# Hedgehog linear attention with a gated unit on one core: tiles 2 and 3 as two pairs of products, four down-weight loads behind the state, and a newly searched order

## The chip, the core and the metric

The kernel runs on one core of a Trainium2 chip. The metric is device time in microseconds (us) of one execution; a kernel's time is the median of its runs. The profile is of one execution, taken by the hardware profiler. A core has five engines with a queue of instructions each: TensorE (PE; its weight loads are PEld), VectorE (DVE), ScalarE (ACT), GpSimd (POOL) and SyncE (SP). Here SP issues nearly all DMAs. Products are collected in PSUM, in eight banks of 128 rows by 512 float32 values, numbered 0 to 7.

## The reference, cut to what matters

One block of a transformer on 2048 tokens of width 448, in bfloat16: an attention without a softmax over tokens (16 heads of 28), and then a gated unit of width 1792. Each half has a layer norm before it and a sum with its input after it.

```python
qkv = layernorm(x) @ wqkv                       # q, k, v: 16 heads, 28 wide
pq, pk = q @ w_phi, k @ w_phi                   # per head, 28 x 28
phi_q = concat(softmax(pq), softmax(-pq))       # over the 28 features
phi_k = concat(softmax(pk), softmax(-pk))
kv = einsum("bhsf,bhsd->bhfd", phi_k, v)        # the state: sums over all 2048 tokens
z  = einsum("bhsf->bhf", phi_k)
o  = (phi_q @ kv) / (phi_q . z + 1e-6)
h  = x + o @ wo
n  = layernorm(h)
out = h + (sigmoid(n @ w_gate) * (n @ w_up)) @ w_down
```

No query can be finished before the state `kv` holds all tokens. That splits the program into a part before the state and a part behind it.

## The kernel before, in words

The tokens are 16 tiles of 128. The kernel is a graph of tasks. A task has a name, an engine, a function that issues its instructions, and the tasks that it depends on. `stored` reads a table `ORDER` that is written in the file: each number holds a task (number divided by 32), the engine that it takes where several are allowed, and which of the allowed PSUM banks it uses. `emit` puts the tasks into the engines' queues in that order, and puts in a wait wherever a task depends on another engine. So nothing is decided at run time: the order of every queue, SP's too, is that of the table. A list `TURNS` adds single dependencies on top, each of one named task on another, all of them of a POOL task on a DVE task. The table came out of a search with a model of the engines; the search isn't part of the file.

The tasks that the change and the prediction speak of, in the order of the data (numbers in brackets are lines of the profile of before; copies by the helper `copy` all have line L432):

- **Loads** (L468), on SP: `x` in pieces (`x0` is tiles 0 and 1, `x2` 2 and 3, on ACT's queue, `x4`, `x6`, then `x8` and `x12` with four tiles each), `wk` (weights of the keys), `wph` (w_phi), `wv` (weights of the values, two halves), `wq` (of the queries, four pieces), `wom` (of the output, eight small pieces), later `wg`, `wu` (gate, up) and `wd` (down, seven pieces).
- **Norm of x**: statistics (`bst` L590, `agg` L592), the power -1/2 on POOL (`rstd` L595), normalised tiles `xn` (L610 on DVE, L609 on ACT). Tiles 0 to 3 are transposed on PE (L620) and copied out; tiles 4 to 15 go as six DMA transposes `xT` (L628), two tiles each.
- **Folded weights**: the key weights are multiplied by w_phi on PE (L547, L562) and copied out by ACT, giving `Wk2`; the same for the queries after two DMA transposes `wqT` (L508), giving `Wq2`. `fill` (L995) are products of zeros that write a bank nobody reads.
- **Keys and values** (L644): a pair of products of 448 columns for two banks. A pair is issued as two tasks, `pa` (8 matmuls) and `pb` (6). An ordinary pair holds keys and values of one tile. For a tile in the list `VV`, the pair `va`/`vb` holds the values of two tiles and `pa`/`pb` their keys. The second task of a pair waits until the first one has ended.
- **Features of the keys**: `ekp`, `ekm` (two exponentials on ACT, L664, L666), `v1` (values copied out), `ss` (sums, DVE, L685), `rs` (reciprocal, L689), `phi` (the product of the two, L691, on POOL or DVE), `kv` (16 matmuls into bank 4, L703), `kvz` (the state copied out of bank 4 by DVE, L758).
- **Queries** (L743): `qa`/`q`, two groups for each of four chunks of four tiles, with exponentials `eqp`, `eqm` on ACT (L753).
- **Output of the attention**, by tile: `num` (L779, 16 matmuls) and `ocp` (copied out). By pair of tiles: `rSm`, `rr`, `b`, `c`, `rd`, `o` on DVE (L795 to L807), `od` (L826), a DMA transpose `oT` (L828; pair 0 on PE with two copies `oT0.0` and `oT0.1`), `woa`/`wo_` (L840), `h` (the sum with x, L870; for pair 0 the copies `hc`), `bst2`/`agg2`, `ve2` and `rstd2` (POOL, L880), the normalised `hn` (L884), and a DMA transpose `hT` (L902; pair 0 on PE). `oT1` is of pair 1 (tiles 2 and 3), and so on.
- **Gated unit**, in five chunks of 2, 4, 4, 4 and 2 tiles, 14 columns of 128 each: `ga`/`gu` (L941, 8 and 6 matmuls; `gu5.1` is column 5 of chunk 1), `sig` (ACT, L950), `hh` (DVE, L958), then by tile `dn` (L975, 14 matmuls), `fin` (DVE, L982) and the store `st` (SP, L985).

Chunk 1 of the gated unit needs `hT1` and `hT2`, chunk 2 `hT3` and `hT4`, chunk 3 (tiles 10 to 13) `hT5` and `hT6`, chunk 4 `hT7`. The last chunk's `dn` close the program.

Of the kernel before, what the change touches and what calls it, by code (L numbers as in the profile page):

```python
# [32 lines left out]
NFILL = 12  # L33
# [53 lines left out]
"""  # L87


TURNS = [(('rstd', 4), ('xn', 3)), (('phi', 0), ('xn', 9)), (('phi', 4), ('xn', 12)), (('phi', 7), ('xn',  # L90
         15)), (('phi', 10), ('phi', 9)), (('phi', 14), ('phi', 13)), (('ve2', 2), ('hn', 3)), (('rstd2', 2),
         ('hn', 3)), (('ve2', 4), ('o', 5)), (('rstd2', 4), ('o', 5)), (('rstd2', 3), ('od', 5)), (('rstd2',
         5), ('od', 7))]


class _Task:
# [232 lines left out]
def build(nc, A_x, A_wqkv, A_w_phi, A_wo, B_w_gate, B_w_up, B_w_down, out):  # L329
    S = A_x.shape[1]  # L330
    NT = S // P
# [17 lines left out]
    with ExitStack() as es:  # L349
# [6 lines left out]
        phi = sb("phi", [P, NPHI, 2, 2 * G, 32, 2])  # L356
# [42 lines left out]
        kvz = sb("kvz", [P, 2, G, E, 2])  # L399
        opm = sb("opm", [P, NOP, 2, 2, G, E, HL])  # L400
        rSm = sb("rSm", [P, 2, 2, G, HL], dt.float32)
        rr = sb("rr", [P, 2, 2, G, HL])
# [633 lines left out]
```

## Time and profile before

| What | Value |
|---|---|
| Time, median of 3 runs (lowest to highest) | 205.77 us (205.53 to 206.45) |
| The profiled execution: its time, its span | 206.47 us, 204.7 us |
| Busy: PE, DVE, ACT, POOL | 196.0, 134.4, 94.7, 33.0 us |
| Granted TensorE clock | 0.998 |
| First pair on DMA-transposed tiles begins | 19.28 us |
| The last `kv` ends, the state is complete | 47.00 us |
| First `ga` of chunk 0, first `ga` of chunk 1 | 65.40, 78.66 us |
| First `dn` | 97.22 us |

The span runs from the first to the last instruction; the time of an execution has 1.77 us more around it here. In the profile a row of the timeline or of the chain begins with the start and the duration in us; a row of a group ends with its busy time in us, the mean duration of one instruction in ns, and the idle time of the engine just before. A matmul of a pair uses half of the rows of the array, and two of them run side by side, so that the busy time of one is about twice what it costs in the queue. Instructions that issue a DMA stand under the queue of their engine (SPq), and the time to landing counts from the start of the issue.

### The profile page before, as it was taken

To read this page: it belongs to the slowest core of one execution; us is meant where nothing else is said; L and a number is where in the kernel's file an instruction comes from. 1 tells how busy PE (TensorE), PEld (TensorE's weight loads), DVE (VectorE), ACT (ScalarE), POOL (GpSimd) and SP (SyncE) were. 2 spreads that over 40 slices of the span, in tenths; PEclk is the share of its full clock that TensorE was granted. 3 is DMA by queue.
4 is the path that set the end of the run, shared out by engine and by line. 5 is a ranking of instruction groups with operands and counts; after the bars stand their busy time and mean duration, and the time that the engine had idled before them with its cause. 6 is when DMAs were issued, how large, how long until landed. Compare 5 with 4: busy or idle time off the path is not lost.

```text
span 204.7 us, 5395 instructions
## 1 busy us (share of the span) xinstructions
PE 196.0 (96%) x2276; PEld 109.5 (53%) x2276; DVE 134.4 (66%) x304; ACT 94.7 (46%) x169; POOL 33.0 (16%) x51
## 2 busy tenths in 40 slices
PE   7996999998889998999999999999999999999994
PEld 2643545555436985554544555454444555786553
DVE  2969989997999995779948846713455313541412
ACT  2698999999999462444031441301334400441000
POOL 5515936570000200003000000110000000000000
PEclk9999999999999999999999999999999999999999
DMA  5999599574040396310260020050020000200041
GB/s 144 317 248 162 161 165 148 159 226 142 3 100 6 80 150 160 96 45 11 52 146 5 0 51 3 0 125 3 0 74 3 2 0 3 69 3 0 30 159 60
DMA packets 35109, 16.94 MB, mean 83 GB/s; under 512 B 26828, under 2 KB 34060, under 8 KB 35084
## 3 DMA queue, kind: packets, MB, share of 16 engines
q1 hardware_dynamic: 34812, 16.36, 35.3%
q8 instruction: 18, 0.29, 0.7%
q10 hardware_dynamic: 272, 0.23, 0.3%
q14 instruction: 7, 0.06, 0.1%
HBM read 8.98 MB, written 1.84 MB: 53 GB/s over the span
## 4 chain that ended last, share of the span: by engine, by line
PE 85%; DMA 5%; DVE 4%; SPq 3%; issue 1%; ACT 0%; DVEq 0%
PE bank L941 42%; PE bank L975 21%; PE bank L644 8%; PE bank L743 5%; PE bank L840 5%; SPq L468 3%; DMA x_sb<-in_A_x_dram 3%; PE bank L703 2%; DMA xnT<-xn_pad 2%; PE bank L779 1%; DVE o_pad L807 1%; DVE opm L432 1%; DVE st L865 1%; ACT opm L432 0%; DVE st L590 0%
## 5 line engine op out<-in xcount | busy, mean ns | idle before, releaser
L941 PE MATMUL bank<-xnT,wg_sb 64*128 64x512 bf16 (+1 forms) x490 | 87.5, 333 | 0.6 <-issue 0.6
L941 PE MATMUL bank<-xnT,wu_sb 64*128 64x512 bf16 (+1 forms) x490 | 87.6, 333 | 0.0
L950 ACT ACTIVATE sg_sb<-bank 128x512 f32<-128x512 f32 (+1 forms) x70 | 34.7, 512 | 81.9 <-PE bank L941 76.1
L958 DVE SCALAR_TENSOR_TENSOR hh<-sg_sb,bank 128x512 bf16<-128x512 f32 (+1 forms) x70 | 39.0, 575 | 30.8 <-ACT sg_sb L950 28.5
L941 PEld LDWEIGHTS bank<-xnT,wg_sb 64*128 64x128 bf16 x490 | 45.0, 94 | 21.3 <-issue 3.5
L941 PEld LDWEIGHTS bank<-xnT,wu_sb 64*128 64x128 bf16 x490 | 44.8, 94 | 14.0
L975 PE MATMUL bank<-wd_sb,hh 128*128 128x448 bf16 (+1 forms) x238 | 43.1, 342 | 0.0
L975 PEld LDWEIGHTS bank<-wd_sb,hh 128*128 128x128 bf16 x238 | 22.9, 98 | 20.1 <-DVE b_sb L799 0.4
L982 DVE SCALAR_TENSOR_TENSOR x_sb<-bank,x_sb 128x448 bf16<-128x448 f32 (+1 forms) x17 | 9.9, 594 | 24.6 <-PE bank L975 24.5
L644 PE MATMUL bank<-Wk,xnT 64*128 64x448 bf16 x112 | 21.7, 350 | 0.3
L644 PE MATMUL bank<-Wv,xnT 64*128 64x448 bf16 x112 | 21.9, 350 | 0.0
L691 POOL TENSOR_TENSOR phi<-ek,rsum 128x896 bf16<-128x896 bf16 x10 | 16.8, 1690 | 9.0 <-DVE xn_pad L610 4.8
L685 DVE TENSOR_REDUCE ssum<-ek 128x32 f32<-128x896 bf16 x16 | 16.6, 1068 | 0.9 <-ACT ek L664 0.7
L753 ACT ACTIVATE eq<-bank 128x1024 bf16<-128x1024 f32 x16 | 16.7, 1068 | 0.2
L880 POOL TENSOR_TENSOR rs<-rs,neghalf 128x2 f32<-128x2 f32 x8 | 5.6, 698 | 59.5 <-DVE rs L878 59.2
L743 PE MATMUL bank<-xnT,Wq 64*128 64x512 bf16 x112 | 14.3, 377 | 0.0
L840 PE MATMUL bank<-wo_sb,oT 64*128 64x448 bf16 x112 | 13.0, 350 | 0.6 <-DVE rs L878 0.6
L432 ACT CAST opm<-bank 128x960 bf16<-128x960 f32 x13 | 12.1, 976 | 1.4 <-PE bank L779 1.4
L644 PEld LDWEIGHTS bank<-Wk,xnT 64*128 64x128 bf16 x112 | 9.2, 94 | 6.0 <-PE bank L644 1.5
L644 PEld LDWEIGHTS bank<-Wv,xnT 64*128 64x128 bf16 x112 | 9.1, 94 | 4.9 <-ACT WkT L432 0.3
L870 DVE TENSOR_TENSOR x_sb<-bank,x_sb 128x896 bf16<-128x896 f32 x7 | 7.5, 1087 | 3.4 <-PE bank L840 3.4
L590 DVE BATCH_NORM_STATS2 st<-x_sb 128x6 f32<-128x448 bf16 x16 | 9.2, 604 | 0.5 <-DMA x_sb<-in_A_x_dram 0.5
(92 smaller groups left out, 168.3 us busy)
## 6 DMA issues: line engine op xcount, KB each, us to landing
wu_sb<-in_B_w_up_dram SPq DMA_DIRECT2D x4, 448.0 KB, 3.8
wg_sb<-in_B_w_gate_dram SPq DMA_DIRECT2D x4, 448.0 KB, 4.8
out_dram<-x_sb SPq DMA_DIRECT2D x15, 112.0 KB, 1.8
wd_sb<-in_B_w_down_dram SPq DMA_DIRECT2D x7, 224.0 KB, 2.8
x_sb<-in_A_x_dram SPq DMA_DIRECT2D x2, 448.0 KB, 5.4
x_sb<-in_A_x_dram SPq DMA_DIRECT2D x3, 224.0 KB, 4.3
wq_raw<-in_A_wqkv_dram SPq DMA_DIRECT2D x4, 128.0 KB, 3.5
Wv<-in_A_wqkv_dram SPq DMA_DIRECT2D x2, 224.0 KB, 4.5
```

The source lines that it names most:

```text
L432: return e.copy(dst, src) if hasattr(e, "activation") else e.tensor_copy(dst, src)
L644: r = e.matmul(bank[bk][:, 0:D], lhsT=half(xnT, hi)[:, t, k, :], rhs=half(w, hi)[:, k, :], start=(i == 0), stop=(i == 6), tile_position=(6 ...
L685: task(("ss", t), "dve", dve(896), lambda e, s=s: e.tensor_reduce(ssum[:, s, :].rearrange("p (a h) -> p a h", h=2), ek[:, s].rearrange("p ...
L691: task(("phi", t), None, 1.68, lambda e, t=t, s=s: e.tensor_tensor(phi[:, t % NPHI, :, :, 0:DH, :].rearrange("p a g d h -> p (a g) d h"), ...
L743: r = e.matmul(bank[bb[j]], lhsT=half(Wq2, hi)[:, k, 2 * g:2 * g + 2].rearrange("p c d h -> p (c d h)"), rhs=half(xnT, hi)[:, 4 * c:4 * c ...
L753: task((key, gp, c), "act", act_p(1024), lambda e, gp=gp, c=c, sg=sg, nm=nm: e.activation(eq[c][:, sg, 2 * gp:2 * gp + 2, :], wide[got(nm) ...
L840: r = e.matmul(bank[bb[j]][:, 0:D], lhsT=half(oT, hi)[:, pr % NO, j, k, :], rhs=half(wo_sb, hi)[:, k, :], start=(i == 0 and not res), stop ...
L941: r = e.matmul(bank[b][:, 0:N], lhsT=half(w, hi)[:, k, fs], rhs=half(hnT, hi)[:, t0:t0 + n, k, :], start=(i == 0), stop=(i == 6), tile_pos ...
L950: task(("sig", f_, c), "act", act_p(N), lambda e, j=j, N=N, nm=nm: e.activation(sg_sb[:, j % NSG, 0:N], bank[got(nm)[0]][:, 0:N], ACT.Tanh ...
L958: task(("hh", f_, c), "dve", dve(N), lambda e, j=j, N=N, nm=nm, f_=f_, c=c: e.scalar_tensor_tensor(hhT[c % 2][:, f_, 0:N], sg_sb[:, j % NS ...
L975: r = e.matmul(bank[b][:, c0:c1], lhsT=hhT[c % 2][:, f_, o:o + P], rhs=wd_sb[:, f_, c0:c1], start=(f_ == 0), stop=(f_ == FT - 1))
L982: task(("fin",) + nm[1:], "dve", dve(c1 - c0), lambda e, nm=nm, tt=tt, pr=pr, c0=c0, c1=c1: e.scalar_tensor_tensor(X(tt)[:, c0:c1], bank[g ...
```

## The change

Four things change in the code, and the table is replaced.

1. `VV` gets tile 2 as a second entry. Tiles 2 and 3 were two ordinary pairs; they become one pair of values (`va2`/`vb2`) and one pair of keys (`pa2`/`pb2`). Two dependencies that named `pb` of a tile now take it from `k_at`, since tile 3 no longer has a `pb` of its own.
2. The loads `wd0` to `wd3` depended on `gu1.0`, `gu3.0`, `gu5.0` and `gu7.0`; now they depend on `kvz`. Each load also waits for the one two places before it in the list of late loads, as before.
3. `NFILL` goes from 12 to 16.
4. `TURNS` has 8 entries in place of 12, of which most are new.
5. `ORDER` is new throughout: engines, banks and places in the queues.

```diff
-NFILL = 12
+NFILL = 16
...
-544 737 0 128 320 1152 448 609 352 27904 480 577 27936 512 768 160 9120 192 640 96 27968 224 288 28000 800 256
...
+544 737 0 224 128 1152 448 577 160 27904 352 609 96 27936 480 640 27968 512 192 256 28000 800 320 384 28032
...
-TURNS = [(('rstd', 4), ('xn', 3)), (('phi', 0), ('xn', 9)), (('phi', 4), ('xn', 12)), (('phi', 7), ('xn',
-         15)), (('phi', 10), ('phi', 9)), (('phi', 14), ('phi', 13)), (('ve2', 2), ('hn', 3)), (('rstd2', 2),
-         ('hn', 3)), (('ve2', 4), ('o', 5)), (('rstd2', 4), ('o', 5)), (('rstd2', 3), ('od', 5)), (('rstd2',
-         5), ('od', 7))]
+TURNS = [(('rstd', 2), ('xn', 1)), (('rstd', 4), ('xn', 2)), (('phi', 1), ('xn', 10)), (('phi', 5), ('xn',
+         15)), (('rstd2', 0), ('rr', 3)), (('rstd2', 2), ('od', 3)), (('rstd2', 1), ('hn', 4)), (('rstd2', 4),
+         ('c', 6))]
...
-        VV = (0,)
+        VV = (0, 2)
...
-                     ("gu", 1 + 2 * j, 0) if name[0] == "wd" else ("pb", 4 + 2 * j + (name[0] == "wu"))])
+                     ("kvz" if j < 4 else ("gu", 1 + 2 * j, 0)) if name[0] == "wd" else ("pb", 4 + 2 * j + (name[0] == "wu"))])
...
-                deps.append(("pb", min(4 * c + 3, NT - 1)))
+                deps.append(k_at[min(4 * c + 3, NT - 1)][2])
...
-            qdone = [("q", gp, c) for gp in range(2)] + [("pb", NT - 1)]
+            qdone = [("q", gp, c) for gp in range(2)] + [k_at[NT - 1][2]]
```

What the new table does to the queues, as far as the prediction speaks of it (before, then after):

```
SP, first loads   x0 wk1 wk0 x4 wph x6 wv1 wv0 wom0 wq3 wq2 wq1 wq0 x8 x12 wqT1 wqT0 xT4 xT6
                  x0 wk0 wk1 wph x6 x4 wq3 wq1 wq2 x8 wq0 wom2 wv1 wv0 x12 wqT1 wom1 wqT0 wom6 xT4 xT6
PE, tiles 0 to 3  va0 .. vb0 .. pa0 pb0 pa3 pb3 pa2 pb2
                  pa0 pb0 pa2 va0 pb2 va2 vb0 vb2
phi on DVE        3 5 8 9 13 15
                  0 2 4 9 10 11 14 15
SP, behind state  oT1 oT2 wd1 oT3 wd3 wd0 hT1 hT2 wd5 oT4 wd2 wd4 wd6
                  wd1 oT1 oT2 oT3 wd0 hT2 hT1 wd2 wd3 wd4 oT4 wd6 wd5
DVE, near chunk 3 hn13 hh8.2 hh10.2 hn12 hn10 fin4
                  hh13.2 hh11.2 hn14 hn15 fin3 hn12 hn13 fin4
SP, near chunk 3  oT7 hT6 hT5 st0 hT7 st1
                  oT7 st0 hT5 st3 st1 hT6 hT7
PE, near chunk 3  dn2 dn4 dn5 dn3, then chunk 3
                  dn2 dn3 dn4 dn5, then chunk 3
```

90 rows, old and new, of the table ORDER are left out of this document.

## The prediction

> **What bounds it now.** I read the busy shares first, then the busy time by stage (cut at the events of the table above), the chain that ended last in order of time, the waits, and last SP's queue and the landings of single DMAs.
>
> ```profile
> PE 196.0 (96%) x2276; PEld 109.5 (53%) x2276; DVE 134.4 (66%) x304; ACT 94.7 (46%) x169; POOL 33.0 (16%) x51
> ```
> ```profile
> 19.28:47.00 27.72, 27.72 (x486) 15.31 (x488) 25.61 (x49) 25.72 (x48) 18.19 (x14) 1.00 0.78 172
> 47.00:65.40 18.40, 16.23 (x330) 8.84 (x332) 17.51 (x41) 17.72 (x22) 0.70 (x1) 1.00 0.22 57
> 65.40:78.66 13.26, 12.64 (x244) 11.18 (x239) 12.45 (x36) 7.43 (x18) 1.59 (x3) 1.00 0.69 130
> 78.66:130.04 51.38, 51.38 (x473) 26.34 (x474) 37.34 (x82) 16.12 (x27) 2.93 (x5) 1.00 0.19 46
> 130.04:140.74 10.70, 10.70 (x58) 5.40 (x60) 3.76 (x9) 0.60 (x1) 0.76 (x2) 1.00 0.26 61
> ```
>
> The columns of the second fence are stretch, length, then busy time and count of PE, PEld, DVE, ACT, POOL. PE is the bound, and it has little left to give. From 19.28 to 47.00 it has no gap at all, and none from 78.66 to 140.74. It idles 18.40 - 16.23 = 2.17 us while the attention's output is begun, and 0.62 us before chunk 1. In those two stages, and from 19.28 on, DVE is nearly as full as PE (25.61 of 27.72, 17.51 of 18.40, 12.45 of 13.26). So DVE decides when the waits there end. PE's work does not change: the same 2 x 7 x 16 matmuls for keys and values, only paired otherwise.
>
> ```profile
> 8.35 5.29 DMA x_sb<-in_A_x_dram
> 14.85 4.39 DMA xnT<-xn_pad
> 78.04 0.62 issue
> 130.04 10.70 PE bank L975 x56
> ```
> ```profile
> PEld bank L644 <- PE bank L644: 1.5, 3, 0.5
> PE bank L562 <- DMA WqT<-wq_raw: 1.5, 1, 1.5
> PE bank L848 <- DVE oT L432: 0.6, 1, 0.6
> PE bank L840 <- DVE rs L878: 0.6, 1, 0.6
> ```
>
> The chain runs over the load x8, the statistics and the transpose xT4, which lands at 19.24; everything behind is PE. Where PE waits, it waits for a DMA transpose or for DVE.
>
> **The pairs of tiles 2 and 3: 0.** The waits show three weight loads that sat 0.5 us each until PE was empty: `pb` directly behind its own `pa`. In the new order only pb0 follows so. That saves two such stops, but ahead of the wait for WqT and xT4 (1.5 us of PE standing still at L562), which goes on as long as those transposes are in flight. Values don't start earlier either: pa0 and pa2 stand before va0, and Wv is now issued 13th and 14th. If the cover were gone, two stops would be worth up to 2 x 0.5 = 1.0 us.
>
> **Four more fills: 0.** They are short, stand in the same idle stretch, and only kT starts behind them; pa0 waits for ACT's copies of Wk2.
>
> **The start: +0.4 us.**
>
> ```profile
> 8.35 1.56 SPq L468 DMA_DIRECT2D x_sb<-in_A_x_dram  x2
> 10.31 4.49 SPq L508 DMA_TRANSPOSE WqT<-wq_raw  x2
> 14.85 3.26 SPq L628 DMA_TRANSPOSE xnT<-xn_pad  x2
> 18.16 1.66 SPq L468 DMA_DIRECT2D wo_sb<-in_A_wo_dram  x2
> ```
>
> x8 moves up four places, some 2 us at 8.35 us for the fourteen it had. That ends DVE's wait for it. But SP is busy without a hole from the WqT transposes into xT4 (10.31 + 4.49 = 14.80, then 14.85), so earlier `xn4` and `xn5` don't bring xT4 forward. Nearly the same bytes stand ahead of the WqT transposes as before. New are two pieces of `wo`: wom1 between the WqT transposes and wom6 between the second one and xT4. One piece costs SP 1.66 / 2 = 0.83 us. wom1 falls where the transposes are held back anyway (4.49 us for two), wom6 does not. Ends: -0.5 (SP is freed sooner, as DVE's wait for x8 was 0.5) and +0.83. I take +0.4, half a piece, since the landing of xT4 followed 4.4 us behind its issue and part of that is the queue of DMAs, not SP. PE has no gap behind 19.28, so this goes through to the state.
>
> **More on DVE before the state: 0, with ends 0 and +1.1.**
>
> ```profile
> L691 POOL TENSOR_TENSOR phi<-ek,rsum x10: 1689/1690/1691, 19.1 to 44.1; 128x896 bf16<-128x896 bf16 x10
> L691 DVE TENSOR_TENSOR phi<-ek,rsum x6: 558/587/834, 29.8 to 45.5; 128x896 bf16<-128x896 bf16 x6
> L432 DVE CAST v<-bank 128x448 bf16<-128x448 f32 x1 | 0.6, 626 | 0.5 <-PE bank L644 0.5
> ```
>
> DVE makes eight `phi` instead of six, and two copies of values instead of one: 2 x 0.587 + 0.626 = 1.8 us more. Its idle time in that stage was 27.72 - 25.61 = 2.1 us. It fits, with 0.3 us over, and phi15 and the last `kv` stay at the end of both queues.
>
> **From the state to chunk 1: -0.3 us.**
>
> ```profile
> L432 DVE CAST opm<-bank 128x960 bf16<-128x960 f32 x3 | 3.5, 1154 | 0.6 <-PE bank L779 0.6
> L432 DVE CAST x_sb<-bank 128x448 bf16<-128x448 f32 x1 | 0.6, 593 | 0.0
> L432 DVE COPY oT<-bank 128x512 bf16<-128x512 bf16 x1 | 0.4, 426 | 0.1
> L958 DVE SCALAR_TENSOR_TENSOR hh<-sg_sb,bank 128x256 bf16<-128x256 f32 x28 | 10.9, 414 | 7.2 <-ACT sg_sb L950 5.5 <-PE bank L975 1.6
> L878 DVE TENSOR_SCALAR rs<-mv 128x2 f32<-128x2 f32 x6 | 1.0, 165 | 0.1
> L880 POOL TENSOR_TENSOR rs<-rs,neghalf 128x2 f32<-128x2 f32 x8 | 5.6, 698 | 59.5 <-DVE rs L878 59.2 <-DVE o_pad L826 0.2
> ```
>
> Up to the last `hn` of tiles 2 to 5 DVE loses ocp8 (1.154) and hc0 (0.593) to ACT and gains oT0.0 (0.426), ve22 (0.165) and one more `hh` (0.414): -0.74. But hn0 now stands directly behind rstd2 of pair 0, which POOL makes in 0.698 and which was filled by ocp8: +0.7, and what stands behind hn0 waits too (hP0 on PE among it). So the last `hn` comes as before.
>
> Its transposes then meet the loads of `wd`:
>
> ```profile
> 71.18 1.05 SPq L468 DMA_DIRECT2D wd_sb<-in_B_w_down_dram  x2
> 72.48 3.88 SPq L902 DMA_TRANSPOSE xnT<-hn_pad  x2
> 132.09 2.59 SPq L902 DMA_TRANSPOSE xnT<-hn_pad  x2
> ```
> ```profile
> L902 SPq DMA_TRANSPOSE xnT<-hn_pad x2: 1231/1896/2561, 72.5 to 73.8; - x2
> ...
> DMA to landing us min/median/max: 4.8/5.0/5.3
> ```
> ```profile
> DMA to landing us min/median/max: 2.8/2.8/2.8
> ```
>
> The second fence is the tile `hn_pad` in 72 to 76 us, the third the same tile in 131 to 134. With two loads just ahead a transpose lands after 4.8 to 5.3 us, with none after 2.8. Now wd1 is issued before oT1 and out of the way, but wd0 still goes directly before hT2 and hT1; the new dependency on `kvz` does not move it, its place in the queue does. One load ahead instead of two is worth 1.05 / 2 = 0.5 us at most; and woa1 takes banks 2 and 3 and so no longer waits for hc0 (the second wait of 0.6 us above, whose named releaser stands directly behind hc0). Ends: -1.2 (both PE waits of 0.6 go) and +0.7 (POOL's 0.698 unpaid). I take -0.3, near the middle. `dn0` has its weights long before; that the loads come earlier is worth 0. wd1 waits on SP for `kvz` and for wu3, with oT1 behind it, but oT1 isn't ready before:
>
> ```profile
> 57.05 3.49 SPq L828 DMA_TRANSPOSE oT<-o_pad  x2
> ```
>
> That is 10 us behind the state: 0.
>
> **Before chunk 3: +0.5 us.**
>
> ```profile
> 135.48 0.62 DVE L982 SCALAR_TENSOR_TENSOR x_sb<-bank,x_sb 128x448 bf16<-128x448 f32 x1 [3.09 <-PE bank L975]
> 131.66 0.73 DVE L884 TENSOR_SCALAR hn_pad<-x_sb,mv,rs 128x512 bf16<-128x512 bf16 x2
> out_dram<-x_sb SPq DMA_DIRECT2D x15, 112.0 KB, 1.8
> ```
>
> So far hT5 and hT6 were issued at 132.09 and landed under the four `dn` (56 matmuls, 10.70 us). Now hn12 and hn13 stand behind fin3 on DVE, and fin3 waits for dn3; behind them wait hT6 and hT7: two `dn` take 10.70 / 2 = 5.35, fin3 0.62, the two `hn` 0.73, together 6.7 us behind the start of dn2; with st3 and st1 ahead on SP hT6 is issued about 7.3 us behind it. Landing after 2.8 us makes 10.1, in time for chunk 3 at 10.7. Landing after 5.3 us makes 12.6, 1.9 late. Ends 0 and +1.9; I take +0.5, because two stores of 112 KB are half of two `wd`.
>
> The Trainium skill (DMA: Bandwidth & Descriptors, Queues, rings and completion order) has each DMA engine take descriptors in ring order, without a barrier between the data of two DMAs. By that alone two stores would hold hT6 back by no more than their own bytes, and this term would be 0 and the sum 0.1. The 5.3 us behind two loads speak for more, so the row stands.
>
> **The sum:** 0 + 0 + 0.4 + 0 - 0.3 + 0.5 = +0.6 us. The profiled execution, 206.47, is 0.70 above the median; I put the 0.6 on the median: 206.4 us. What a measurement of this kernel can tell from no change is about 0.5%, 1.03 us.
>
> **Rivals.**
>
> *Slower, by hT6 (0.23).* If the transpose behind st3 and st1 lands after 5.3 us, PE stands 1.9 us before chunk 3, with the start's 0.4 and the -0.3: 207.8. For it speaks the landing behind `wd`; against it that stores land in 1.8. It decides from a landing of about 4.3 us on.
>
> *Slower, by POOL and DVE (0.15).* phi15 took 0.834 instead of 0.558 us:
>
> ```profile
> 44.14 1.69 POOL L691 TENSOR_TENSOR phi<-ek,rsum 128x896 bf16<-128x896 bf16 x1 [1.16 <-DVE phi L691]
> 45.47 0.83 DVE L691 TENSOR_TENSOR phi<-ek,rsum 128x896 bf16<-128x896 bf16 x1
> ```
>
> POOL's `phi` ran until 45.83, and DVE's ended 0.47 behind that. The turns that kept phi10 and phi14 on POOL behind DVE's are gone, and DVE has two more. One DVE `phi` that comes just behind POOL's start would stand up to 1.69 us; with 0.3 to spare this moves the state by 1.4: 205.77 + 0.6 + 1.4 = 207.8. Against it: by the new order POOL has no `phi` beside most of DVE's. The Trainium skill (SBUF — State Buffer, Who interferes with whom) says that a DVE instruction with two SBUF inputs and a GpSimd one that reads SBUF shut each other out for a whole instruction; by that rule the full 1.69 is possible, and the one row agrees.
>
> *Faster (0.20).* All transposes land in 2.8 us and DVE's -0.74 counts: the start -0.5, the stage before chunk 1 -1.2, chunk 3 nothing: 205.77 - 1.7 = 204.1.
>
> *As summed (0.42)*: 206.4, its own range 205.0 to 206.8. It holds too if the change does nothing, the tables being worth the same.
>
> **Range and chances.** From the faster case, 204.1, to the two slower ones, 207.9; beyond lie both slower ones together or a wait that I don't see. Faster by over 0.5%: 0.20; within: 0.42; slower: 0.38.
>
> **What would show it.** PE's first pair on xT4 near 19.7 us; the last `kv` ending at 47.2 to 47.6; hT1 and hT2 landing after 4 to 5 us and a PE wait under 0.6 before chunk 1; PE idle 0 to 1 us between dn5 and chunk 3, with hT6 landing. I am wrong if xT4 lands before 18.8, if a `phi` on DVE takes over 1 us before the state, or if PE waits in chunks 1 and 2 for a bank that `hh` holds.

## The result, and the profile after

The changed kernel takes 208.75 us (median of 19 executions, 206.47 to 210.81), the kernel before 206.28 us in the same comparison: ratio 1.0103, 95% interval 1.0079 to 1.0127. It is slower by 1% (by the medians 2.47 us, 1.2%), where +0.6 us (0.3%) and a range of 204.1 to 207.9 us were forecast. The ratios here and below leave out executions that stand over 1.5% above the fastest of their kernel; the medians count all, and the profiled execution of the changed kernel is the slowest of its 19 (210.81 us).

First the granted clock in 40 slices and the stages of the changed kernel, cut at the same events as before (stretch, length, busy time and count of PE, PEld, DVE, ACT, POOL, then the granted clock).

```profile
PEclk9999999999997899999999999999999999999999
```
```profile
19.83:47.74 27.91, 27.91 (x486) 15.15 (x488) 24.68 (x46) 24.09 (x46) 14.57 (x11) 1.00 0.73 185
47.74:68.53 20.79, 17.88 (x313) 9.01 (x314) 16.33 (x39) 18.21 (x22) 0.70 (x1) 0.93 0.17 39
68.53:83.03 14.50, 13.12 (x259) 10.83 (x254) 13.32 (x39) 7.95 (x18) 1.39 (x2) 0.98 0.58 84
83.03:136.55 53.52, 53.52 (x493) 24.57 (x494) 38.56 (x83) 15.85 (x27) 2.44 (x5) 1.00 0.26 56
136.55:147.25 10.70, 10.70 (x58) 5.40 (x60) 4.36 (x9) 1.08 (x2) 1.36 (x2) 1.00 0.29 73
```

All of the difference of the two profiles is made by 83.03 us: from the first `ga` of chunk 1 to the end it is 209.1 - 83.03 = 126.07 us here and 204.7 - 78.66 = 126.04 before. Ahead of it stand +0.55 us up to the first pair on xT4, +0.19 from there to the state, +2.39 up to chunk 0 and +1.24 in chunk 0. The waits of PE and the chain say where:

```profile
PE bank L839 <- DMA oT<-o_pad: 2.1, 2, 1.8
PE bank L643 <- DMA xnT<-xn_pad: 1.4, 1, 1.4
PE bank L940 <- DMA xnT<-hn_pad: 1.4, 1, 1.4
```
```profile
14.72 5.07 DMA xnT<-xn_pad
60.58 4.69 DMA oT<-o_pad
77.99 5.00 DMA xnT<-hn_pad
```

Three transposes landed late, and PE stood for each of them. The second is the strange one. oT2 took 4.69 us where it took 2.73 before, with no load near it. The DMA view of 61.6 to 65.3 us (queue, kind: packets, MB, share; then issues with the time to landing) has one packet that no instruction of the kernel issued:

```profile
GB/s 0 22 163 277 291 288 291 291 468 268 271 236 67 6 0 0 0 0 0 0 0 0 0 0 3 8 8 8 11 8 8 11 8 0 0 0 0 0 0 0
...
q1 hardware_dynamic: 1056, 0.26, 32.4%
q8 instruction: 1, 0.02, 2.5%
...
oT<-o_pad SPq DMA_TRANSPOSE x1, 4.7
```

Its kind is "instruction": 16 KB of the program's own code. In the trace it starts at 62.42 us and takes 1.48 us. The transpose is at full rate until then (slices of 291 GB/s), stands still for 1 us, and drips out at 8 GB/s. Such packets come through the whole run of both kernels: 18 in the profile of before, the first with 229 and the last with 4516 of PE's matmuls and weight loads begun, so one per (4516 - 229) / 17 = 252 of them. That they are PE's code is inferred from this count. The one that came nearest in the profile of before, at 62.09 us, began just behind oT2's landing.

Behind the wait for oT2 the clock fell: eight matmuls of 448 columns took 1.29 us there and 0.93 in the like place at 61.12 us.

```profile
61.12 0.93 PE L839 MATMUL bank<-wo_sb,oT 64*128 64x448 bf16 x8 [0.25 <-DMA oT<-o_pad]
...
65.32 1.29 PE L839 MATMUL bank<-wo_sb,oT 64*128 64x448 bf16 x8 [1.80 <-DMA oT<-o_pad]
```

### The profile page after: what moved, and what is told of

Its sections match the earlier page's. It is cut to its first block, busy times and chain, and to the rows that moved or that the text cites. A ratio compares the mean times of both kernels' runs of the same rounds, so it can differ in the third digit from the quotient of the medians.

```text
span 209.1 us, 5402 instructions
## 1 busy us (share of the span) xinstructions
PE 198.2 (95%) x2280; PEld 107.4 (51%) x2280; DVE 135.0 (65%) x304; ACT 94.4 (45%) x169; POOL 30.0 (14%) x51
## 4 chain that ended last, share of the span: by engine, by line
PE 81%; DMA 9%; DVE 7%; ACT 2%; issue 0%
PE bank L940 40%; PE bank L974 20%; PE bank L643 8%; PE bank L742 5%; PE bank L839 4%; DVE st L589 3%; DMA xnT<-xn_pad 2%; DMA xnT<-hn_pad 2%; PE bank L702 2%; DMA oT<-o_pad 2%; ACT opm L431 2%; DMA x_sb<-in_A_x_dram 1%; DVE xn_pad L609 1%; PE bank L778 1%; DVE o_pad L806 1%; DVE mv L591 1%
## 5 line engine op out<-in xcount | busy, mean ns | idle before, releaser
L949 ACT ACTIVATE sg_sb<-bank 128x512 f32<-128x512 f32 (+1 forms) x70 | 34.2, 511 | 80.2 <-PE bank L940 77.8
L940 PEld LDWEIGHTS bank<-xnT,wg_sb 64*128 64x128 bf16 x490 | 45.5, 94 | 24.1 <-issue 2.3
L940 PEld LDWEIGHTS bank<-xnT,wu_sb 64*128 64x128 bf16 x490 | 45.4, 94 | 14.8
L643 PE MATMUL bank<-Wk,xnT 64*128 64x448 bf16 x112 | 20.5, 350 | 1.5 <-DMA xnT<-xn_pad 1.4
L643 PE MATMUL bank<-Wv,xnT 64*128 64x448 bf16 x112 | 20.4, 350 | 0.0
L431 ACT CAST opm<-bank 128x960 bf16<-128x960 f32 x14 | 13.2, 982 | 7.2 <-PE bank L778 7.2
L839 PE MATMUL bank<-wo_sb,oT 64*128 64x448 bf16 x112 | 14.2, 369 | 2.2 <-DMA oT<-o_pad 2.1
L690 POOL TENSOR_TENSOR phi<-ek,rsum 128x896 bf16<-128x896 bf16 x8 | 13.4, 1690 | 13.6 <-ACT ek L665 4.8
L663 ACT ACTIVATE ek<-bank 128x448 bf16<-128x448 f32 x16 | 8.7, 557 | 3.2 <-PE bank L643 3.1
```

What stands on the lines that cost most here:

```text
L431: return e.copy(dst, src) if hasattr(e, "activation") else e.tensor_copy(dst, src)
L643: r = e.matmul(bank[bk][:, 0:D], lhsT=half(xnT, hi)[:, t, k, :], rhs=half(w, hi)[:, k, :], start=(i == 0), stop=(i == 6), tile_position=(6 ...
L690: task(("phi", t), None, 1.68, lambda e, t=t, s=s: e.tensor_tensor(phi[:, t % NPHI, :, :, 0:DH, :].rearrange("p a g d h -> p (a g) d h"), ...
L839: r = e.matmul(bank[bb[j]][:, 0:D], lhsT=half(oT, hi)[:, pr % NO, j, k, :], rhs=half(wo_sb, hi)[:, k, :], start=(i == 0 and not res), stop ...
L940: r = e.matmul(bank[b][:, 0:N], lhsT=half(w, hi)[:, k, fs], rhs=half(hnT, hi)[:, t0:t0 + n, k, :], start=(i == 0), stop=(i == 6), tile_pos ...
L949: task(("sig", f_, c), "act", act_p(N), lambda e, j=j, N=N, nm=nm: e.activation(sg_sb[:, j % NSG, 0:N], bank[got(nm)[0]][:, 0:N], ACT.Tanh ...
```

## The experiments

The first theory, "code": a packet of code among a transpose's packets delays it, and where it falls depends on how many instructions PE has ahead. Its rival, "loads", is the prediction's: a load issued just ahead delays it. A third theory, "clock", came out of the first runs. The table has, from each profile, the first pair on xT4, the end of the last `kv` and the first `ga` of chunk 1 (us); then PE's two waits ahead of that first pair (for WqT, for xT4), the executions whose mean granted clock was 0.992 or less, the median and the ratio to the kernel before. The kernel before ran beside each group of experiments too, with medians of 205.78 to 206.12 us; its 101 executions of the column "low clock" are these.

| Kernel | xT4 | state | chunk 1 | waits | low clock | median | ratio (95%) |
|---|---|---|---|---|---|---|---|
| before | 19.28 | 47.00 | 78.66 | 1.53, 0.1 | 6 of 101 | 206.28 | 1 |
| changed | 19.83 | 47.74 | 83.03 | 0.83, 1.45 | 11 of 19 | 208.75 | 1.0103 |
| e10, changed again | 19.82 | 49.20 | 80.62 | 0.90, 1.34 | 3 of 6 | 208.59 | 1.0145 (1.0103 to 1.0187) |
| e1, 12 fills | 20.23 | 49.83 | 81.14 | 0.86, 1.41 | 4 of 6 | 208.49 | 1.0107 (1.0068 to 1.0146) |
| e2, wd0 early | 19.78 | 47.69 | 78.65 | 1.02, 1.34 | 7 of 12 | 208.12 | 1.0054 (1.0015 to 1.0093) |
| e3, 136 instructions more | 18.95 | 46.86 | 77.25 | 0, 0.53 | 1 of 12 | 204.97 | 0.9957 (0.9935 to 0.9978) |
| e4, wom behind | 19.87 | 47.78 | 79.51 | 1.34, 0.76 | 1 of 12 | 206.85 | 1.0036 (1.0011 to 1.0060) |
| e5, six products in the wait | 21.09 | 49.01 | 79.42 | 1.54, 0 | 0 of 12 | 206.28 | 1.0036 (1.0014 to 1.0058) |
| e7, e3 and e4 together | 17.98 | 45.90 | 76.28 | 0, 0 | 1 of 9 | 204.53 | 0.9925 (0.9891 to 0.9960) |
| e11, 40 instructions more | 19.73 | 49.33 | 80.33 | 0.9, 1.3 | 5 of 12 | 207.76 | 1.0067 (1.0036 to 1.0099) |
| e6, before, 160 more | 18.11 | 45.99 | 78.59 | 0, 0 | 0 of 12 | 205.53 | 0.9984 (0.9951 to 1.0017) |
| e8, before, wd early | 19.20 | 46.91 | 77.78 | 1.2, 0 | 1 of 12 | 205.17 | 0.9959 (0.9928 to 0.9990) |
| e9, before, wd early, 88 more | 19.11 | 46.83 | 77.84 | 0.2, 0.7 | 1 of 12 | 205.90 | 1.0007 (0.9982 to 1.0032) |
| e12, before, wom ahead | 20.76 | 50.16 | 81.24 | 2.51, 0.58 | 5 of 12 | 206.84 | 1.0029 (1.0001 to 1.0056) |

### Fills and loads: e1, e2

e1 drops the last four fills from the table; e2 moves one number of it.

```diff
-NFILL = 16
+NFILL = 12
```
```
SP, e2   ... wd1 wd0 oT1 oT2 oT3 hT2 hT1 ...
```

> The changed kernel with twelve fills as before in place of sixteen; nothing else is moved. Theory 'code': in the traces a packet of 16 KB of the kind 'instruction' comes after about every 250 matmuls and weight loads of PE, and in the changed kernel one came at 62.42 us, while oT2's packets were moving, which then landed 4.69 us behind its issue (2.73 before, with no such packet). Four fills are 8 of PE's matmuls and weight loads; with these gone the packet comes later by what PE does in 8 instructions, about 0.5 us there, at the end of oT2's packets (62.75): oT2 lands in 2.7 to 3.3 us, PE's wait of 1.8 us before woa2 is near zero, the granted clock is 0.998 or more, first ga of chunk 0 near 66, ratio to the kernel before 1.002 to 1.007 in place of 1.010. Theory 'loads' (a transpose lands late behind loads that are issued just ahead of it): oT2 had none ahead and fills are nothing to it, so this run is as the changed kernel, ratio 1.008 to 1.013.

> The changed kernel with wd0 issued directly behind wd1, ahead of oT1, so that no load stands ahead of hT2 and hT1. Theory 'loads': both land 2.7 to 2.9 us behind their issue in place of 5.0 to 5.5, PE's wait of 1.4 us before chunk 1 goes, ratio 1.003 to 1.005. Theory 'code': the packet of instructions that came at 79.33 us is still there, since PE's instructions are the same: one of hT2 and hT1 still lands after 4 us or more, and PE's wait before chunk 1 stays within 0.5 us of 1.4; ratio 1.008 to 1.013.

e1: oT2 landed after 2.72 us, as "code" had it, and the time stayed where it was, which "code" had not: the clock now fell behind the wait for xT4. The early landing of oT2 can't be put down to the fills: in e10, the changed kernel as it is, oT2 landed after 2.73 us as well, with the packet at 66.42 us (66.44 in e1). The fills themselves are worth nothing that shows.

e2: with no load ahead hT2 and hT1 still landed after 4.87 and 4.21 us, with a packet of code at 75.30. "Loads" as the sole cause has fallen. Its ratio lies between the two forecasts: its oT2 landed after 2.73 us, since the packet that had met it came at 64.31 in this execution. By the medians e2 is 2.2 us above the kernel before beside it (208.12 and 205.94), with the low clock in 7 of its 12. From e2's DMA view of 72.8 to 78.7 us:

```profile
q8 instruction: 1, 0.02, 1.0%
...
xnT<-hn_pad SPq DMA_TRANSPOSE x2, 4.5
```

### Moving the packets: e3, e11

Four of the fills become short products, 18 each in e3 and 6 each in e11 (SHORT = 6).

```diff
+SHORT = 18
...
+                if i < 4:
+                    for _ in range(SHORT):
+                        r = e.matmul(bank[5][:, 0:16], lhsT=warm[:], rhs=warm[:, 0:16], start=True, stop=True)
+                    return r
```

> The changed kernel with four of the sixteen fills replaced by 18 products of 16 columns each: 68 matmuls and 68 weight loads more at the very start of PE's queue, 136 instructions, in a stretch where PE waits for loads. Theory 'code': every packet of 16 KB comes 136 of PE's instructions earlier: the one of 62.42 us at about 58 us, ahead of oT1's packets (59.5), the one of 79.33 us at 73.5 to 75 us, between oT3's issue and its packets. So oT1, oT2, hT2 and hT1 all land 2.7 to 3.0 us behind their issue though wd0 is still issued directly ahead of hT2, PE doesn't wait for oT2 or before chunk 1 for more than 0.5 us together, the clock is 0.998 or more, ratio 0.994 to 1.002. Theory 'loads': hT2 and hT1 still land after 4.4 us or more, ratio 1.003 to 1.013.

> The changed kernel with four fills replaced by 6 short products each, 40 of PE's instructions more at the start, in place of the 136 that brought 0.9957. Theory 'code': it is not the short products that help but where the packets fall; with 40 more the packet that came at 62.4 to 64.4 us comes 1 to 2 us earlier, so that it meets oT2's packets (61.7 to 62.8) in nearly every execution: oT2 lands after 4 us or more, PE stands 1 to 2 us ahead of woa2, ratio 1.009 to 1.018. If short products help in themselves (a clock kept whole, or PE's start), the ratio is 0.994 to 1.002.

e3 turned the loss into a gain: 0.9957, with 136 instructions of PE *added*. The packets did not come where I had put them (53.76, 64.82, 69.80 and 77.15 us), but none met oT1, oT2, hT2 or hT1: 2.75, 2.72, 3.38 and 2.99 us to landing. From 72.4 to 76.8 us, with wd0 still directly ahead of hT2:

```profile
q1 hardware_dynamic: 2742, 0.88, 92.6%
issues: line engine op xcount, KB each, median us to landing
wd_sb<-in_B_w_down_dram SPq DMA_DIRECT2D x2, 224.0 KB, 4.9
xnT<-hn_pad SPq DMA_TRANSPOSE x2, 3.2
```

At the start too: the packet of 14.72 us had stood among the WqT transposes; e3's came at 9.87 and 20.49, and PE's first pair began 0.9 us earlier. e11 has the same products, fewer of them. It met oT2 at its beginning (packet 62.39, landing 3.21 us), is slower than before (1.0067) and has the low clock again. So short products do not help in themselves; but the hit was weaker than I had expected, and where the packets fall moves by 2 us and more from one execution to another.

### The start and the clock: e4, e5, e10, e12

e4 and e12 move pieces of `wo` on SP; e5 adds six products of zeros, which stand directly ahead of `pa4` in the table; e10 is the changed kernel.

```
SP, e4    wqT1 wqT0 xT4 xT6 wom1 wom6
SP, e12   wqT1 wqT0 wom5 wom2 xT4 xT6      (the kernel before)
```
```diff
+        for i in range(6):
+            task(("keep", i), "pe", 0.22, lambda e: e.matmul(
+                bank[4][:, 0:448], lhsT=warm[:], rhs=x_sb[:, 0, :], start=False, stop=False, skip_group_check=True),
+                ["kv0", x_ld[0]])
```

> The changed kernel with the two pieces of wo (wom1 and wom6) issued behind xT6 in place of among the WqT transposes and xT4. The prediction's step on the start: SP is freed sooner for xT4, PE's first pair on it begins near 19.3 us in place of 19.83, the last kv ends near 47.2 in place of 47.74; PE's instructions are the same, so a packet of instructions still meets oT2's packets in many executions, and the ratio comes down by 0.5 us at most, to 1.007 to 1.010. If xT4 is held back by something else than SP (the packet of 16 KB at 14.72 us, or the DMAs' bytes): first pair still 19.7 to 19.9, ratio 1.008 to 1.013.

> The changed kernel with six products of zeros more (448 columns, added to bank 4, where they change nothing) between the fold of the query weights and the first pair on xT4: PE works through most of the 1.45 us in which it stood there. Theory 'clock': in the run with twelve fills the granted clock fell to half right behind that wait (a matmul of 448 columns took 0.58 us in place of 0.36 from 20.65 us on) and cost about 1.7 us; the changed kernel does so in about half of its executions and the kernel before hardly ever, and that is the larger part of its 1%. Then with PE busy there the clock stays whole and the ratio is 1.002 to 1.006 in place of 1.010, with oT2 still late in some executions. Rival: the clock falls behind the wait for oT2 (65.3 us in the changed kernel's profile) and not here; then the ratio stays at 1.008 to 1.013.

> The changed kernel, as it is, beside the other two on one chip. From what the runs showed: the clock falls to half behind the wait for xT4 or for oT2 in about half of the executions (time 208.5 to 210.8) and stays whole in the others (206.5 to 208.4); ratio 1.008 to 1.013. In its profile either the matmuls of 448 columns take 0.58 us behind one of the two waits, or the clock is whole and the time is under 208.4 us. oT2 lands after 2.7 us if the packet comes near 64.3 us, as in the runs with wd0 early and with wom behind, and after 4.7 us if it comes near 62.4.

> The kernel before with two pieces of wo (wom5 and wom2) issued ahead of xT4 in place of behind xT6, some 1.3 us of SP (1.66 us for the two by the profile of before). PE's wait behind the fold of the query weights, 0.1 us so far, becomes 1.0 to 1.5 us, as in the changed kernel; all else is the kernel before. Theory 'clock': that wait alone makes the granted clock fall to half behind it in a good part of the executions (mean clock 0.992), so that these lose 1.7 us more than the later start: first pair on xT4 at 20.2 to 20.6 us, ratio 1.006 to 1.015, the times in two groups. If the clock falls in the changed kernel for some other reason (its PE order, its fills): the clock stays whole and the ratio is 1.003 to 1.006, the later start alone. If xT4 is held back by the DMAs' own queue and not by SP: first pair still near 19.3, ratio 0.998 to 1.002.

e10's profile shows what the first one of the changed kernel hid. PE waits 0.90 us, works 0.77, waits 1.34, and then its pairs follow at 0.37 us in place of 0.19:

```profile
17.71 0.77 PE L561 MATMUL bank<-Wp,WqT 112*128 112x112 bf16 x12 [0.90 <-DMA WqT<-wq_raw]
19.82 0.55 PE L643 MATMUL bank<-Wk,xnT 64*128 64x448 bf16 x1 [1.34 <-DMA xnT<-xn_pad]
...
20.16 0.58 PE L643 MATMUL bank<-Wk,xnT 64*128 64x448 bf16 x1
...
20.54 0.58 PE L643 MATMUL bank<-Wk,xnT 64*128 64x448 bf16 x1
```
```profile
19.82:49.20 29.38, 29.38 (x486) 15.59 (x488) 24.84 (x46) 24.20 (x46) 14.71 (x11) 0.95 0.67 176
49.20:80.62 31.42, 29.46 (x568) 18.80 (x568) 28.77 (x78) 26.14 (x39) 2.09 (x3) 1.00 0.35 63
```

The same 486 matmuls take 29.38 us in place of 27.91, without a gap: 1.47 us for one such fall (1.69 in e1). The ratio of e10, 1.0145, is a little above its forecast. A fall did not come in every execution. Of the 19 of the changed kernel 11 have the low clock, with a median of 209.50 us; the other 8 have 207.24. The mean clock of an execution doesn't tell where its fall was: in the profiled one it was behind oT2, in e10, e1, e11 and e12 at the wait for xT4.

e5 puts work into the second wait, and the fall is gone from all 12 executions, though xT4 landed later (21.05) in its profile:

```profile
19.24 0.76 PE L565 MATMUL bank<-Wp,WqT 112*128 112x112 bf16 x12 [1.54 <-DMA WqT<-wq_raw]
19.84 1.30 PE L1003 MATMUL bank<-x_sb,warm 128*128 128x448 bf16 x6
21.09 0.36 PE L647 MATMUL bank<-Wk,xnT 64*128 64x448 bf16 x1
```

e12 makes the opposite test: the kernel before, which has the low clock in 6 of 101 executions (0 of the 17 beside e12), gets it in 5 of 12 by a longer start alone. Its stretch up to the state:

```profile
20.76:50.16 29.40, 29.40 (x486) 15.83 (x488) 24.98 (x47) 25.26 (x47) 17.57 (x14) 0.94 0.57 159
```

The ratio of e12, 1.0029, leaves most of those five out, and is lower than "clock" expected; its median is 1.0 us up. The table's two columns go together: with two waits of 2.2 us and more in sum, 0.8 us apart, the clock falls in between 5 of 12 and 4 of 6 executions; with 2.1 (e4) or less, in at most 1 of 9. (In e12's profile the long wait is the one for WqT, 2.51 us, which a packet at 17.09 had met; more than the order on SP made it.)

The clock record in the traces says what counts. In the 13 profiles that have one the granted clock changes only in steps of 3.41 us, and where the steps lie against the kernel's start differs from one execution to the next. Each fall behind a wait lasts one step, so that PE loses 3.41 / 2 = 1.7 us at most. Over the 752 whole steps of these profiles PE was busy for 1.62 us or less in seven (two of them at the kernel's end), and the step behind each of the seven has half the clock; in all others it was busy for 1.79 us or more, and the clock stayed. First two steps of e10, then the emptiest step of the kernel before ahead of its end (columns as above, then the share and the rate of the DMAs):

```profile
16.00:19.41 3.41, 1.58 (x22) 0.80 (x16) 3.38 (x9) 3.16 (x8) 0.15 (x1) 1.00 1.10 174
19.41:22.83 3.42, 3.01 (x18) 1.26 (x20) 3.42 (x10) 1.01 (x2) 2.08 (x3) 0.50 0.63 131
```
```profile
16.35:19.76 3.41, 1.79 (x24) 1.00 (x22) 3.38 (x9) 2.73 (x7) 2.18 (x5) 1.00 0.77 159
```

So the idle time within one step decides, and not the longest wait. Whether two waits lie in one step is chance: e2's profile has them too (1.02 and 1.34 us), but a step ended within the first, at 17.54 us, the next still had 1.94 us of work, and the clock stayed whole.

e4 also answers the prediction's step on SP. Without the two pieces of `wo` xT4 was issued at 14.83 us and landed at 19.82, no earlier; a packet (16.17 us) stood among the transposes. What e4 gained, it gained by the clock: its executions with a whole clock have a median of 206.79 us, 1.0 above the kernel before, as those of the changed kernel.

### How good are the two tables? e6, e7, e8, e9

e6 is the kernel before with e3's edit (SHORT = 21); e7 is e3 with e4's order; e8 is the kernel before with the second part of the change alone; e9 is e8 with SHORT = 12.

```
SP, e8   ... wu3 wd0 wd1 wd2 wd3 oT1 oT2 oT3 hT1 hT2 ...
```

> The kernel before with four of its twelve fills replaced by 21 products of 16 columns each, 160 of PE's matmuls and weight loads more at the start. Theory 'code': the packet of instructions that came at 74.22 us, among hT1's packets, comes ahead of them, so hT1 and hT2 land 2.7 to 3.4 us behind their issue (5.3 and 4.8 before) though wd3 and wd0 still stand directly ahead; the one of 15.72 us is gone from the WqT transposes and xT4 lands some 0.5 us earlier; PE's wait of 0.62 us before chunk 1 goes; ratio 0.992 to 0.997. Within 0.3% of the changed kernel with short products (0.9957), the two tables are worth the same and the packets made the difference; under 0.992 the new table itself is slower; about 1.000 the new table itself is the faster. Theory 'loads': hT1 and hT2 still land after 4.4 us or more, ratio 0.997 to 1.002.

> The changed kernel with the short products (136 instructions of PE more at the start) and with wom1 and wom6 behind xT6. With the packets of instructions out of the way SP's time should count: in the run with short products xT4 was issued at 15.63 us and PE waited 0.53 us for it. Two pieces of 0.6 us less on SP: xT4 issued near 14.5, no wait of PE before the first pair on it, 0.5 us gained: ratio 0.991 to 0.994. If SP's order counts for nothing there: as with the short products alone, 0.9957.

> The kernel before with one part of the change alone: wd0 to wd3 wait for kvz and are issued behind wu3, ahead of oT1; nothing else moves. Theory 'loads', the prediction's: hT1 and hT2 land after 2.7 to 2.9 us, PE's waits before chunk 1 (0.62 us) go, ratio 0.996 to 0.998. Theory 'code': the packet that came at 74.22 us still meets hT1, which lands after 4.2 us or more; ratio 0.999 to 1.002.

> The kernel before with wd0 to wd3 issued ahead of oT1 (as in the run of that part alone, 0.9959) and four fills replaced by 12 short products each, 88 of PE's instructions more at the start. In the run with 160 more the packets came at 69.51 and 76.26 us and the second met hT2; with 72 fewer they should come some 2 us later, near 71.5, between oT3's packets and hT1's. Theory 'code': start 1.0 us earlier as in that run (state near 46.0), hT1 and hT2 land after 2.7 to 3.0 us, no wait of PE before chunk 1; ratio 0.988 to 0.993, as good as the best of the changed kernel (0.9925): then the two tables are worth the same and all of the loss lies in packets and clock. If it stays at 0.995 or above with no packet among oT2, hT1 and hT2, the new table itself is the faster one.

e7 has the best ratio, 0.9925 (its interval overlaps e3's): it beats both kernels, and now SP's order does count (xT4 issued at 14.48 in place of 15.63, no wait ahead of the first pair).

```profile
17.98:45.90 27.92, 27.92 (x486) 15.44 (x488) 26.62 (x51) 25.90 (x50) 14.72 (x11) 1.00 0.71 188
45.90:76.28 30.38, 29.28 (x568) 18.93 (x570) 27.77 (x75) 25.56 (x39) 2.08 (x3) 1.00 0.29 67
```

e6 gained 1.0 us at the start (state at 45.99) and lost it again: the next packet came at 76.26, among hT2's packets, which landed after 4.75 us; 0.9984 in place of the forecast 0.992 to 0.997. In e9 hT1 and hT2 were clean, but one packet (57.74) met oT1, which landed after 4.33 us, and one (12.56) WqT; 1.0007 in place of 0.988 to 0.993. I could not free the kernel before at all places at once, so a like run to e7 is missing. By pieces: the kernel before has 27.72 us from the first pair to the state and 30.87 to 31.01 from there to chunk 1 (e8, e9), the new table 27.92 and 30.38. That makes the new table some 0.3 to 0.4 us better where nothing disturbs it, argued from stages of different runs and not measured: a packet still met hT1 and hT2 in e8 and oT1 in e9, so the kernel before may be held too low.

e8 was faster than "loads" had it, with a packet still there (74.23), and hT1 and hT2 between the forecasts. Seven of these profiles sort the two causes (us from issue to landing of the first and the second `hT`):

| | no packet of code among them | a packet |
|---|---|---|
| no load directly ahead | 2.80, 2.79 (e9) | 4.87, 4.21 (e2); 4.47, 3.90 (e8) |
| loads directly ahead | 3.38, 2.99 (e3); 3.29, 2.87 (e7) | 5.53, 5.00 (changed); 5.26, 4.76 (before) |

A load ahead costs 0.1 to 0.9 us, a packet of code 1.1 to 2.2. In e1, e4, e10 and e12, which have both too, the two land after 4.2 to 5.3 us; in e5, e6 and e11 only one of the two `hT` was fully met.

## Why the prediction was wrong

**The start, +0.4: the term that failed.** The step that failed is "this goes through to the state": it counts a longer wait for xT4 once and puts the clock at nothing. The wait grew from 0.1 to 1.45 us, behind one of 0.83 for WqT. With two such waits the granted clock falls to half for one step of 3.41 us in about half of the executions, which costs 1.5 to 1.7 us (e10, e1; e5 takes the fall away, e12 brings it to the kernel before). The quoted clock column was 1.00 everywhere before, and the working never asked what would become of it; the kernel before, with 1.79 us of work in the step that ends at 19.76, stood just clear of a fall.

The size of the term was met (19.83, +0.55), its cause was not. SP was not later: xT4 was issued at 14.72 us, before at 14.85, and landed after 5.07 us in place of 4.39. Moving the pieces of `wo` away did not bring it forward (e4). A packet of code stood among the transposes there; where none does, xT4 lands 3.27 to 3.33 us behind its issue (e3, e6, e7), and only then the pieces of `wo` count. But the kernel before had such a packet too (15.72 us), so what makes up the 0.55 stays open.

**From the state to chunk 1, -0.3.** Where no packet meets oT2 the size was met, 31.42 us in e10 against 31.66 before, -0.24, but in part by luck: PE's two waits of 0.6 us for `oT` and `rs` went, one of which the working had counted on, while hT2 and hT1 still landed after 5.02 and 4.48 us and PE's wait before chunk 1 grew from 0.62 to 0.87. In the profiled execution a packet did, and the stretch took 35.29. The working blamed the two `wd` loads for landings of 4.8 to 5.3 us; they are the smaller part (the table above). A packet of code was in that very window of the profile of before, in a row that I did not read.

**The pairs, the fills, DVE before the state: 0, 0, 0.** 27.91 us against 27.72 without a gap, the 0.19 unexplained; e1 for the fills. DVE was not fuller but emptier in that stage, 24.68 us in place of 25.61: it has the two more `phi`, but one of them, one of the two copies of values and more of the norm's statistics fell ahead of the stage. The two last `phi` on DVE took 1.09 us for both, so the rival of POOL and DVE did not come:

```profile
45.72 1.09 DVE L690 TENSOR_TENSOR phi<-ek,rsum 128x896 bf16<-128x896 bf16 x2
```

**Before chunk 3, +0.5: it was 0.** The `dn` have no gap (10.70 of 10.70 us), and hT6 and hT7, issued behind two stores, landed as if alone. From 143 to 147.8 us:

```profile
out_dram<-x_sb SPq DMA_DIRECT2D x1, 112.0 KB, 1.8
xnT<-hn_pad SPq DMA_TRANSPOSE x2, 2.8
```

The rival of hT6 fell with it. By the rule that the prediction weighed (the Trainium skill, DMA: Bandwidth & Descriptors, Queues, rings and completion order) this term was 0, and the trace agrees: 2.76 us. I had set the row of before above it, and that row carried a packet of code.

**The account.** The median is up 2.47 us. Executions with a whole clock are up by 207.24 - 206.28 = 0.96, where 206.28 is of all executions of the kernel before. Of this 0.55 is the start and 0.19 the stretch to the state, by the profile; a late oT2 or hT in some of them can give the rest, which is not shown. The others stand 2.26 us higher; one fall explains 1.5 to 1.7 of that, the rest stays open. None of the prediction's three signs of being wrong came, and neither of its two slower rivals.

## What to carry to other kernels

In this kernel the DMA transposes that end critical waits share the DMA engines with the program's own code. In a kernel like it, look for the packets of the kind "instruction" in the window of each late transfer before a neighbouring load is blamed, and try a few instructions more at a place where the engine idles anyway. A wait of PE is not worth its length alone: where two waits lie within a few us and sum up to some 2 us, as here, count a fall of the clock too, and try to fill one with products that change nothing. A time that falls in two groups, with the granted clock beside it, says so sooner than one profile does.

## What the runs showed that was not expected

- One packet of 16 KB, on one queue, holds a transpose of 0.26 MB up for 1.1 to 2.2 us, more than the loads of 224 KB directly ahead of it do. The packets come with PE's progress, but not at one fixed instruction: in the changed kernel the one near oT2 came at 62.42 us, and in e2 and e4, the same on PE, at 64.31 and 64.40.
- The clock fell behind a longest wait of 1.34 us (e10). The Trainium skill (TensorE: Matmul & The Clock Gate, HAM oscillation — how this bites in real kernels) asks for no gap above about 3.4 us; the runs disagree: two waits of 2.24 us in sum with 0.77 us of work between were enough in about half of the executions. The Trainium skill (TensorE: Matmul & The Clock Gate, What's actually happening) has the window run freely, and the traces agree: the steps of 3.41 us lie elsewhere in each execution, so that the fall comes by chance.
- Adding 136 instructions to the engine that bounds the kernel took its ratio to the kernel before from 1.0103 to 0.9957.
